# Regrouping the sums of a spectral layer by part, with changes to the order of statistics, evictions and weight preparation

## The chip, the cores and the metric

The kernel runs on one core of one Trainium2 chip. The metric is the device time of one execution in microseconds; the time before is the median of three runs. A profile is one further execution, recorded instruction by instruction. Its time and its span (first to last instruction) are given beside each other below.

The engines are named as in the profile: PE is TensorE's matmuls and PEld its weight loads, DVE is VectorE, ACT is ScalarE, POOL is GpSimd, SP is SyncE, which here only issues DMAs. Each engine runs its instructions in the program's order; semaphores hold an instruction until another engine, or an earlier operation of its own engine, has finished.

## The reference

Two layers over `x` of 2048 rows by 576 columns in bf16, each behind a layer norm without parameters:

```python
h  = x + irfft2(rfft2(layernorm(x)) * (w_r + 1j * w_i), s=(2048, 576))
h2 = h + (gelu(layernorm(h) @ w_gate) * (layernorm(h) @ w_up)) @ w_down
```

The first multiplies the two-dimensional spectrum of the normalised input (2048 by 289, real input) by a complex weight and transforms back. The second is a gated feed-forward layer with 4608 inner columns. `B_x` is not used.

## The kernel before

The core keeps `x` in SBUF as `h_sb`, 128 partitions by 16 rows `h` by 576 columns, so that sequence row 16p + h lies at partition p. The Fourier transform over 2048 rows is split into a part of 16 and a part of 128; the transforms are matmuls with tables of sines and cosines that the kernel makes itself. The source fixes the order of the instructions on every engine; nothing reorders them.

*Head (to about 25 us).* `x` comes in six DMAs (L72 to 74): rows 0-1, 2-3, 4-5, 6-7, 8-11, 12-15. POOL makes index tables (`iota`), DVE and ACT the row table `F16` (L204 to 220, 273 to 279). Row statistics for the first layer norm come from DVE (`sd`, three instructions a row, L117 to 119) for some rows and from ACT (`ln_act`, two passes with accumulation, L124) for the others; `ln_fin` and `ln_rstd` (L128 to 134) finish them on POOL, four rows at a time. `norms(lo, hi)` writes the normalised rows `xn` on DVE (L137) and issues the first transform of each row on PE (`row16`, L298 and L311, into PSUM tiles `f2t` and `f4`). In front of rows 0, 8 and 12 and of the group `pt`, `fill` issues 14, 8, 5 and 3 matmuls whose result is not used (L286). `evict` and `evict4` copy PSUM into `Bt` (L322, L328): all on ACT but the last `evict4`, which DVE does. The column tables `DT`, `DF`, `DI`, `DS` and the tables `TF` (minus sine, cosine, sine for each of nine channels) and its transpose `TI` are made in between. `first` is the part of `TF` for the first two channels, `rest` the part for the other seven.

*Channel loop (25 to 58 us).* `order` lists eight channels k: 1 to 7, then 0. In turn i:

- `f2(c)` transforms columns for c = k and k + 8 (six matmuls, L478) and copies the result to `pq[c]` (L486, ACT; DVE for c = 9).
- `f3(k, half)` combines `pq[k]` and `pq[k + 8]` with `TF` (L493, L494) into `g` (half 0) and `hs` (half 1), copied by ACT (L514).
- `sums_of(k)` makes difference and sum of `g` and `hs` on DVE, `xab` (L523, 524).
- `wmul(k)` multiplies `xab` by the weights `WR` and `WI` (`m1`, `m2`, L541), combines them to `za` and `zb` (L547, 548), and writes the two halves of `Zt` (L552, 553). `sums_of` of the next channel stands between the last two steps. `za`, `zb`, `m1` and `m2` have one buffer each.
- `i3(k, s)`, s = 0, 1, 2, multiplies slices of `Zt` by `TI` (L569, L571; L592 for k = 0) and ACT copies the result to `EO` (L573, L578).

`f2`, `f3` and `i3` take PSUM tiles of one pool, `two`, with four buffers. PE's order in one turn is `f2(k)`, `f3(.,0)`, `i3(.,0)`, `f3(.,1)`, `i3(.,1)`, `f2(k+8)`, `i3(.,2)`, each for a different channel. In the last turn `inv_cols(0, 0)` (L618) stands in place of `f2`, and all three parts of `i3` follow `f3`.

*Weights.* Spectrum rows 0 to 8 of `WR` and `WI` come by DMA (L154), the mirrored rows by an indirect DMA of POOL into `wm` (L381). `WR`'s mirrored part is then copied by a DMA (L411); `WI`'s by DVE with the factor -1 (L452). DVE halves columns 0 and 288 of both (L454).

*Rest.* `inv_cols`, `add_rows`, a second layer norm, and from 72.6 us the feed-forward layer: 144 blocks of 18 matmuls (L876), a Gelu on ACT (L884), a product on DVE (L885), and the down projection (L896).

Of the kernel before, what the change touches and what calls it, by code (L numbers as in the profile page):

```python
# [20 lines left out]
P = 128  # L21
# [20 lines left out]
def kernel_body(  # L42
# [29 lines left out]
    chunks = ((0, 2), (2, 4), (4, 6), (6, 8), (8, 12), (12, 16))  # L72
# [113 lines left out]
    iota(q16[:], [[16, P]])  # L186
# [10 lines left out]
    for t in range(3):  # L197
# [10 lines left out]
    fs = tmp("fs", [P, P], FP32)  # L208
    A.activation(
        fs[:], mu[:].rearrange("p c l -> p (c l)"), ACT.Sin, bias=npib[:], scale=2.0 * PI / P  # L210
    )
    ia, s2a, s2p = tmp("ia", [P, 1]), tmp("s2a", [P, 1], FP32), tmp("s2p", [P, 1], FP32)
    V.tensor_scalar(ia[:], ip[:], 7, None, op0=ALU.bitwise_and)
    V.tensor_scalar(s2a[:], ia[:], 127.0 / 8.0, None, op0=ALU.mult)
    V.scalar_tensor_tensor(s2p[:], ip[:], 0.125, s2a[:], op0=ALU.mult, op1=ALU.add)
    ks = tmp("ks", [P, 9], FP32)
    V.tensor_scalar(ks[:], kv[:], s2p[:, 0:1], None, op0=ALU.mult)
    V.tensor_scalar(iu[:], iu[:], 7, None, op0=ALU.bitwise_and)
    mask = tmp("mask", [P, P], FP32)
    V.tensor_scalar(mask[:], iu[:].rearrange("p c l -> p (c l)"), 0.0, None, op0=ALU.is_equal)  # L220
# [98 lines left out]
    def evict(*hs):  # L319
        for h in hs:  # L320
            n = 1 if h >= H - 2 else 2
            A.copy(  # L322
                Bt[:, 0:4, :].rearrange("p t (c h l) -> p (t c) h l", c=16, h=16)[:, :, h : h + n, :],
                ps_f[h][:, 0:n].rearrange("p h (tc l) -> p tc h l", l=8),
            )

    def evict4(h):
        (V.tensor_copy if h == 12 else A.copy)(  # L328
            Bt[:, 4, :].rearrange("p (c h l) -> p h c l", c=16, h=16)[:, h : h + 4, :, :],
            ps_f["f4", h][:, 0].rearrange("p (h c l) -> p h c l", h=4, c=16),  # L330
        )
# [55 lines left out]
    G.memset(DF[:], 0.0)  # L387
    ln_fin(slice(9, 12, 2))
    sd(8, 10)
# [5 lines left out]
    norms(8, 12)  # L395
    sd(15)
    ln_fin(slice(13, 14))
    ln_rstd(rstd, mv, 12, 16)
# [26 lines left out]
    evict(12, 14, 15)  # L425
# [3 lines left out]
    evict4(12)  # L429
# [19 lines left out]
    sine(rest)  # L449

    def weights():
        V.tensor_scalar(WI[:, 9 : H + 1, 0:J], wm[1][:].rearrange("p (r j) -> p r j", r=8), -1.0, None, op0=ALU.mult)  # L452
        for w in (WR, WI):
            V.tensor_scalar(w[:, :, 0 : J : J - 1], w[:, :, 0 : J : J - 1], 0.5, None, op0=ALU.mult)  # L454

# [4 lines left out]
    pq = {}  # L460
    xab = {}
# [9 lines left out]
    def f2(c):  # L471
        ps = two("pq_ps")
        col = slice(slot[c] * P, (slot[c] + 1) * P)
        steps = [(par, t) for par in range(2) for t in (par, par + 2, 4)]
        if c == order[0]:
            steps.sort(key=lambda s: s[1] == 4)
        for par, t in steps:
            T.matmul(  # L478
                ps[:, par, 0:JP],
                lhsT=Bt[:, t, col],  # L480
                rhs=DT[:, t // 2, par] if t < 4 else DF[:, par],
                start=(t == par),
                stop=(t == 4),
            )
        sb = wk.tile([P, 2, JP], BF16, name="pq", tag="pq", bufs=6)
        (V.tensor_copy if c == 9 else A.copy)(  # L486
            sb[:].rearrange("p r (j a) -> p r j a", a=2),
            ps[:, :, 0:JP].rearrange("p a (r j) -> p r j a", r=2),
        )
        pq[c] = sb  # L490
# [34 lines left out]

    def wmul(k, i, nxt=None):
        x = xab[k]
# [5 lines left out]
        if k:  # L533
            za, zb = (wk.tile([P, 2, JP], BF16, name=n, tag=n, bufs=1) for n in ("za", "zb"))
        else:
            za, zb = zv[:, 0], zv[:, 1]

        for j0, j1 in ((0, J),) if k else ((0, P), (P, J)):
            js = slice(j0, j1)
            for w, m in ((WR, m1), (WI, m2)):  # L540
                V.tensor_tensor(  # L541
                    m[:, :, :, js],
                    x[:, :, :, js],
                    w[:, sl, js].unsqueeze(1).to_broadcast([P, 2, 2, j1 - j0]),
                    ALU.mult,
                )
            V.tensor_tensor(za[:, :, js], m1[:, 0, :, js], m2[:, 1, :, js], ALU.subtract)  # L547
            V.tensor_tensor(zb[:, :, js], m1[:, 1, :, js], m2[:, 0, :, js], ALU.add)
            if nxt:
                sums_of(nxt)  # L550
            if k:
                V.tensor_tensor(zv[:, 0, :, js], za[:, :, js], zb[:, ::-1, js], ALU.add)  # L552
                V.tensor_tensor(zv[:, 1, :, js], zb[:, :, js], za[:, ::-1, js], ALU.subtract)
# [408 lines left out]
```

## Time and profile before

| | us |
|---|---|
| median of 3 runs (503.38 to 503.83) | 503.68 |
| the profiled execution | 503.36 |
| its span | 501.3 |
| PE, DVE, ACT, POOL busy | 491.3, 211.3, 152.6, 28.5 |
| first matmul that is used (L298) starts | 9.10 |
| first column transform (L478) starts | 25.11 |
| first feed-forward matmul (L876) starts | 72.59 |

In a line of the timeline the columns are start, duration, engine, source line, operation, the tile written `<-` the tiles read, shapes, and the number of instructions merged; a bracket gives idle time before it and what ended it. A line of the chain that ended last has start, duration, engine, tile, line. Durations of neighbouring operations overlap a little, so that the distance from start to start is the better measure of cost. The busy time of PE is modelled, and a matmul that waits for its operands inside the engine may count as busy.

### The profile page before, as it was taken

To read this page: it belongs to the slowest core of one execution; us is meant where nothing else is said; L and a number is where in the kernel's file an instruction comes from. 1 tells how busy PE (TensorE), PEld (TensorE's weight loads), DVE (VectorE), ACT (ScalarE), POOL (GpSimd) and SP (SyncE) were. 2 spreads that over 40 slices of the span, in tenths; PEclk is the share of its full clock that TensorE was granted. 3 is DMA by queue.
4 is the path that set the end of the run, shared out by engine and by line. 5 is a ranking of instruction groups with operands and counts; after the bars stand their busy time and mean duration, and the time that the engine had idled before them with its cause. 6 is when DMAs were issued, how large, how long until landed. Compare 5 with 4: busy or idle time off the path is not lost.

```text
span 501.3 us, 9901 instructions
## 1 busy us (share of the span) xinstructions
PE 491.3 (98%) x4340; PEld 290.9 (58%) x4340; DVE 211.3 (42%) x420; ACT 152.6 (30%) x269; POOL 28.5 (6%) x75
## 2 busy tenths in 40 slices
PE   7999999999999999999999999999999999999996
PEld 3567765555567754444477744444677544444775
DVE  8999766788640125433310145333210233333001
ACT  8999972222320012323200032333100133232000
POOL 8500010111110000000000000000000000000000
PEclk9999999999999999999999999999999999999999
DMA  8539686799950049998800099988300688870000
GB/s 283 172 72 198 183 236 160 152 168 189 178 102 1 1 107 184 193 190 155 158 9 0 7 210 203 195 159 151 74 0 1 144 159 159 154 143 1 12 13 26
DMA packets 88104, 61.46 MB, mean 123 GB/s; under 512 B 22781, under 2 KB 86653, under 8 KB 88061
## 3 DMA queue, kind: packets, MB, share of 16 engines
q1 hardware_dynamic: 87773, 59.65, 60.2%
q0 software_dynamic: 288, 1.18, 0.7%
q8 instruction: 34, 0.56, 0.5%
q14 instruction: 9, 0.07, 0.0%
HBM read 52.65 MB, written 2.36 MB: 110 GB/s over the span
## 4 chain that ended last, share of the span: by engine, by line
PE 93%; DVE 3%; ACT 2%; POOL 1%; issue 0%; POOLq 0%
PE gu L876 56%; PE acc L896 28%; PE cs_ps L618 2%; PE pq_ps L478 2%; PE y_ps L741 1%; PE eo_ps L571 1%; PE eo_ps L569 1%; PE gh_ps L494 1%; DVE xn L137 1%; ACT cwb L631 1%; PE gh_ps L493 1%; PE f2t L298 0%; ACT DT L347 0%; ACT Bt L322 0%; POOL kd L198 0%
## 5 line engine op out<-in xcount | busy, mean ns | idle before, releaser
L876 PE MATMUL gu<-Bt,wgu 64*128 64x512 bf16 x2592 | 281.5, 376 | 0.8 <-ACT cwb L631 0.8
L876 PEld LDWEIGHTS <-wgu 64*128 64x128 bf16 x2592 | 130.9, 94 | 148.2 <-issue 1.8
L884 ACT ACTIVATE g_sb<-gu 128x512 f32<-128x512 f32 x144 | 86.0, 597 | 302.8 <-PE gu L876 302.8
L885 DVE TENSOR_TENSOR P_sb<-g_sb,gu 128x512 bf16<-128x512 f32 x144 | 98.6, 685 | 152.9 <-ACT g_sb L884 152.9
L896 PEld LDWEIGHTS <-P_sb 128*128 128x128 bf16 x1152 | 112.4, 98 | 30.6 <-issue 2.4
L896 PE MATMUL acc<-wd,P_sb 128*128 128x288 bf16 x768 | 99.3, 286 | 0.0
L908 DVE TENSOR_TENSOR h_sb<-h_sb,acc 128x576 bf16<-128x576 bf16 x15 | 11.3, 754 | 118.2 <-PE acc L896 118.2
L896 PE MATMUL acc<-wd_a,P_sb 128*128 128x288 bf16 x384 | 52.3, 286 | 0.5 <-DVE h_sb L904 0.5
L478 PE MATMUL pq_ps<-DT,Bt 128*128 128x290 bf16 x64 | 12.2, 286 | 0.0
L286 PE MATMUL f2t<-h_sb,ident 128*128 128x512 bf16 x27 | 8.6, 479 | 3.7 <-DMA h_sb<-in_A_x_dram 3.7
L766 DVE TENSOR_SCALAR hrow<-h_sb,mv,rstd 128x1152 bf16<-128x1152 bf16 x14 | 12.1, 866 | 0.0
L134 POOL TENSOR_TENSOR rstd<-rstd,mhalf 128x1 f32<-128x1 f32 (+1 forms) x16 | 11.4, 713 | 1.3
L618 PEld LDWEIGHTS <-EO 128*128 128x128 bf16 x96 | 9.1, 96 | 3.0 <-issue 0.2
L478 PEld LDWEIGHTS <-Bt 128*128 128x128 bf16 x96 | 9.3, 97 | 2.4
L486 ACT CAST pq<-pq_ps 128x580 bf16<-128x580 f32 x15 | 9.8, 662 | 0.4 <-PE pq_ps L478 0.2
L133 POOL TENSOR_SCALAR rstd<-mv 128x1 f32<-128x1 f32 (+1 forms) x16 | 3.8, 238 | 107.3 <-DVE mv L119 107.0
L298 PE MATMUL f2t<-F,xn 128*128 128x256 bf16 x64 | 9.3, 275 | 0.7 <-DVE xn L137 0.7
L124 ACT ACTIVATE junk<-h_sb 128x576 bf16<-128x576 bf16 x14 | 9.4, 676 | 0.5 <-DMA h_sb<-in_A_x_dram 0.5
L118 DVE BATCH_NORM_STATS2 st<-h_sb 128x6 f32<-128x288 bf16 x21 | 9.3, 441 | 0.0
L117 DVE BATCH_NORM_STATS2 st<-h_sb 128x6 f32<-128x288 bf16 x21 | 9.3, 441 | 0.0
L618 PE MATMUL cs_ps<-DI,EO 128*128 128x290 bf16 x32 | 9.1, 285 | 0.0
L493 PE MATMUL gh_ps<-pq,TF 128*128 128x289 bf16 x32 | 8.7, 286 | 0.3 <-ACT TF L256 0.3
(132 smaller groups left out, 248.8 us busy)
## 6 DMA issues: line engine op xcount, KB each, us to landing
wgu<-in_B_w_gate_dram SPq DMA_DIRECT2D x48, 432.0 KB, 5.3
wgu<-in_B_w_up_dram SPq DMA_DIRECT2D x48, 432.0 KB, 6.8
wd<-in_B_w_down_dram SPq DMA_DIRECT2D x2, 1728.0 KB, 7.5
wd_a<-in_B_w_down_dram SPq DMA_DIRECT2D x1, 1728.0 KB
out_dram<-h_sb SPq DMA_DIRECT2D x3, 576.0 KB, 3.4
h_sb<-in_A_x_dram SPq DMA_DIRECT2D x4, 288.0 KB, 3.2
h_sb<-in_A_x_dram SPq DMA_DIRECT2D x2, 576.0 KB, 6.3
WR<-in_A_w_r_dram SPq DMA_DIRECT2D x1, 650.2 KB
```

The source lines that it names most:

```text
L124: A.activation(junk[:], h_sb[:, h, :], fn, scale=sc, accum_out=mv[:, h, i : i + 1])
L134: G.tensor_tensor(dst[:, sl], dst[:, sl], mhalf[:, sl], ALU.pow)
L478: T.matmul(ps[:, par, 0:JP], lhsT=Bt[:, t, col], rhs=DT[:, t // 2, par] if t < 4 else DF[:, par], start=(t == par), stop=(t == 4),)
L486: (V.tensor_copy if c == 9 else A.copy)(sb[:].rearrange("p r (j a) -> p r j a", a=2), ps[:, :, 0:JP].rearrange("p a (r j) -> p r j a", r=2),)
L493: T.matmul(dst, lhsT=TF[:, ts[k1], t0, :], rhs=a, start=True, stop=False)
L618: T.matmul(ps[:, e, 0:JP], lhsT=EO[x][:, 2 * e + jt if jt < 2 else 4, 2 * g : 2 * g + 2].rearrange("p h e k l -> p (h e k l)"), rhs=DI[:, ...
L766: V.tensor_scalar(hrow[:], h_sb[:, h, :].rearrange("p (r k) -> p r k", k=64).unsqueeze(2).to_broadcast([P, NR, 2, 64]), mv2[:, h, 0:1], rs ...
L876: T.matmul(gu[:, c, :], lhsT=w[rows, r, i * P : (i + 1) * P], rhs=hl[tcnk % 2][rows, r, :], start=(r == 0), stop=(r == NR - 1),)
L884: A.activation(g_sb[:], gu[:, 0, :], ACT.Gelu_apprx_tanh)
L885: V.tensor_tensor(p_sb(fa + i), g_sb[:], gu[:, 1, :], ALU.mult)
L896: T.matmul(acc[:, c, 0:DH], lhsT=p_sb(f)[:, st * P : (st + 1) * P], rhs=wd[f // NWA][:, f % NWA, cc], start=(f == 0), stop=(f == NFT - 1),)
L908: V.tensor_tensor(hv, hv, acc[:, :, 0:DH], ALU.add)
```

## The change

The diff has these parts.

1. *Input.* The first DMA of `x` is split in two, rows 0 and 1 (seven DMAs in all).
2. *Row table.* ACT makes three sine tables (the third with the opposite sign) in two instructions, and one DVE operation compares and multiplies, where a mask, a product and a negation stood. The scaling of `q16`, `s2p`, `ks` is spread otherwise, with two small DVE operations fewer.
3. *Order of statistics.* ACT takes row 0 in place of row 1, DVE rows 1, 2, 4, 6 and 8 ahead of `norms(0, 4)`, where it took 0, 2, 4 and 6. `sd(10)` is left of `sd(8, 10)`. `ln_rstd(12, 16)` is done in three pieces, row 13 last; the memset of `DF` and `minus_sine(first)` move.
4. *Late evictions.* `evict(14)` goes to DVE, `evict4(12)` to ACT.
5. *Weights.* `WI`'s mirrored part is copied by a DMA like `WR`'s; no factor -1. POOL, not DVE, halves the two columns, in the head.
6. *Pairing by part.* Each half of `f3` makes, for one of the two parts r, the pair that was spread over both halves; the signs that this turns are those that the factor -1 had turned. The two `Zt` operations of a channel now write columns `zv[:, :, 0]` and `zv[:, :, 1]`, and the parts s of `i3` use these in turn: s = 0 reads only the first.
7. *One operation moved.* The second `Zt` operation of a channel is held back and issued behind the two weight products of the next channel (`held`, `release`).
8. *Order in a turn.* `f2` no longer copies; `f2_out` does. PE's order is `f2(k)`, `f3(.,0)`, `i3(.,0)`, `f3(.,1)`, `f2(k+8)`, `i3(.,1)`, `i3(.,2)`. DVE copies `pq[9]` in two halves. `sine(rest)` moves behind the copy of `pq[1]`, and the copy of `pq[2]` behind `f3(1, 1)`.

The core of it:

```diff
-    chunks = ((0, 2), (2, 4), (4, 6), (6, 8), (8, 12), (12, 16))
+    chunks = ((0, 1), (1, 2), (2, 4), (4, 6), (6, 8), (8, 12), (12, 16))
...
     def row_table():
-        V.tensor_tensor(
-            F16[:, 0:2, :],
-            fs[:].unsqueeze(1).to_broadcast([P, 2, P]),
-            mask[:].unsqueeze(1).to_broadcast([P, 2, P]),
-            ALU.mult,
-        )
-        V.tensor_scalar(F16[:, 2, :], F16[:, 0, :], -1.0, None, op0=ALU.mult)
+        V.scalar_tensor_tensor(
+            F16[:],
+            iu[:].rearrange("p c l -> p (c l)").unsqueeze(1).to_broadcast([P, 3, P]),
+            0.0,
+            fs[:],
+            op0=ALU.is_equal,
+            op1=ALU.mult,
+        )
...
-    ln_act(1)
+    ln_act(0)
     ln_act(3)
-    sd(0)
     row_table()
-    sd(2)
-    ln_fin(slice(1, 4, 2))
+    sd(1, 2)
+    ln_fin(slice(0, 4, 3))
     ln_rstd(rstd, mv, 0, 4)
-    sd(4, 6)
+    sd(4, 6, 8)
     norms(0, 4)
...
-    sd(8, 10)
+    sd(10)
...
     norms(8, 12)
+    minus_sine(first)
+    G.memset(DF[:], 0.0)
     sd(15)
+    ln_rstd(rstd, mv, 12, 13)
+    ln_rstd(rstd, mv, 14, 16)
     ln_fin(slice(13, 14))
-    ln_rstd(rstd, mv, 12, 16)
+    ln_rstd(rstd, mv, 13, 14)
...
-    nc.sync.dma_start(WR[:, 9 : H + 1, 0:J], wm[0][:].rearrange("p (r j) -> p r j", r=8))
+    for w, t in ((WR, wm[0]), (WI, wm[1])):
+        nc.sync.dma_start(w[:, 9 : H + 1, 0:J], t[:].rearrange("p (r j) -> p r j", r=8))
+    for w in (WR, WI):
+        G.tensor_scalar(w[:, :, 0 : J : J - 1], w[:, :, 0 : J : J - 1], 0.5, None, op0=ALU.mult)
...
-    evict(12, 14, 15)
+    evict(12, 15)
+    evict4(12)
...
-    evict4(12)
+    evict(14, copy=V.tensor_copy)
...
-        for r in range(2):
-            if half:
-                comb(ps[:, 1 - r, 0:J], k, C, q[:, r, 0:J], NS, p[:, r, 0:J])
-            else:
-                comb(ps[:, r, 0:J], k, C, p[:, r, 0:J], SN, q[:, r, 0:J])
+        r = half
+        comb(ps[:, r, 0:J], k, C, p[:, r, 0:J], SN, q[:, r, 0:J])
+        comb(ps[:, 1 - r, 0:J], k, C, q[:, r, 0:J], NS, p[:, r, 0:J])
...
+    def release(n):
+        for _ in range(min(n, len(held))):
+            V.tensor_tensor(*held.pop(0))
...
+        if k:
+            times(WR, m1, js)
+            times(WI, m2, js)
+            release(1)
+            za, zb = (wk.tile([P, 2, JP], BF16, name=n, tag=n, bufs=1) for n in ("za", "zb"))
+            parts(za, zb, js)
+            held.append((zv[:, :, 0, js], za[:, :, js], zb[:, ::-1, js], ALU.add))
+            held.append((zv[:, :, 1, js], zb[:, :, js], za[:, ::-1, js], ALU.subtract))
             if nxt:
                 sums_of(nxt)
-            if k:
-                V.tensor_tensor(zv[:, 0, :, js], za[:, :, js], zb[:, ::-1, js], ALU.add)
-                V.tensor_tensor(zv[:, 1, :, js], zb[:, :, js], za[:, ::-1, js], ALU.subtract)
+                release(1)
+            return
...
-        if i >= 3 and not last:
-            i3(order[i - 3], 1)
         if not last and i:
             f2(order[i] + 8)
+            f2_out(order[i] + 8)
         if i >= 3:
-            for jt in range(0 if last else 2, NJT):
+            for jt in range(0 if last else 1, NJT):
                 i3(order[i - 3], jt)
```

More of the change, by code (lines that the diff above doesn't have):

```diff
@@ L185, in kernel_body @@
     q16 = tmp("q16", [P, P], FP32)
-    iota(q16[:], [[16, P]])
+    iota(q16[:], [[2, P]])
     make_identity(nc, ident[:])
@@ L207, in kernel_body @@
     V.tensor_scalar(mu[:], mu[:], 127, None, op0=ALU.bitwise_and)
-    fs = tmp("fs", [P, P], FP32)
-    A.activation(
-        fs[:], mu[:].rearrange("p c l -> p (c l)"), ACT.Sin, bias=npib[:], scale=2.0 * PI / P
-    )
[L212 to L215, printed above, removed]
+    fs = tmp("fs", [P, 3, P], FP32)
+    for n, bias, sign in ((slice(0, 2), npib, 1.0), (slice(2, 3), pib, -1.0)):
+        A.activation(
+            fs[:, n],
+            mu[:].rearrange("p c l -> p (c l)").unsqueeze(1).to_broadcast([P, n.stop - n.start, P]),
+            ACT.Sin,
+            bias=bias[:],
+            scale=sign * 2.0 * PI / P,
+        )
+    V.tensor_scalar(iu[:], iu[:], 7, None, op0=ALU.bitwise_and)
+    s2p = tmp("s2p", [P, 1], FP32)
+    V.scalar_tensor_tensor(s2p[:], iu[:, 0, 0:1], 127.0, ip[:], op0=ALU.mult, op1=ALU.add)
     ks = tmp("ks", [P, 9], FP32)
[L217 to L220, printed above, removed]
+    V.tensor_scalar(ks[:], kv[:], s2p[:, 0:1], 0.125, op0=ALU.mult, op1=ALU.mult)
     def drop_sign(dst, src):
@@ L317, in row16_rest, with evict @@
             )
-    def evict(*hs):
+    def evict(*hs, copy=A.copy):
         for h in hs:
             n = 1 if h >= H - 2 else 2
-            A.copy(
+            copy(
                 Bt[:, 0:4, :].rearrange("p t (c h l) -> p (t c) h l", c=16, h=16)[:, :, h : h + n, :],
@@ L327, in evict4 @@
     def evict4(h):
-        (V.tensor_copy if h == 12 else A.copy)(
+        A.copy(
             Bt[:, 4, :].rearrange("p (c h l) -> p h c l", c=16, h=16)[:, h : h + 4, :, :],
@@ L386, in kernel_body @@
         )
-    G.memset(DF[:], 0.0)
     ln_fin(slice(9, 12, 2))
-    sd(8, 10)
+    sd(10)
     ln_rstd(rstd, mv, 8, 12)
@@ L448, in kernel_body @@
         )
[L449 to L454, printed above, removed]
     xn_pool.__exit__(None, None, None)
@@ L460, in kernel_body @@
     pq = {}
+    pq_ps = {}
     xab = {}
@@ L484, in f2, with f2_out @@
             )
[L485 to L488, printed above, removed]
+        pq[c] = wk.tile([P, 2, JP], BF16, name="pq", tag="pq", bufs=6)
+        pq_ps[c] = ps
+    def f2_out(c, copy=A.copy, rs=slice(0, 2)):
+        copy(
+            pq[c][:, rs].rearrange("p r (j a) -> p r j a", a=2),
+            pq_ps[c][:, :, 0:JP].rearrange("p a (r j) -> p r j a", r=2)[:, rs],
         )
-        pq[c] = sb
     def comb(dst, k1, t0, a, t1, b):
@@ L524, in sums_of @@
         V.tensor_tensor(x[:, 1, ::-1, 0:J], g[:, :, 0:J], hs[:, :, 0:J], ALU.add)
+    held = []
+    def release(n):
+        for _ in range(min(n, len(held))):
+            V.tensor_tensor(*held.pop(0))
     def wmul(k, i, nxt=None):
@@ L650, in kernel_body @@
             f2(order[i])
+            if i != 1:
+                f2_out(order[i])
         if i == 0:
+            sine(rest)
             f2(order[0] + 8)
+            for r in range(2):
+                f2_out(order[0] + 8, V.tensor_copy, slice(r, r + 1))
             angle_c(rest)
             minus_sine(rest)
-            weights()
         if last:
@@ L665, in kernel_body @@
             if i == 1:
+                f2_out(order[1])
                 sums_of(order[0])
```

29 lines of the change are left out of this document (15 added, 14 removed).

## The prediction

> **What bounds the kernel now.** I read the list of cores first (granted clock 1.000, so no throttling to explain), then the busy shares, the chain that ended last, the timeline by stage, and the landing times of the input.
>
> ```profile
> span 501.3 us, 9901 instructions
> ...
> PE 491.3 (98%) x4340; PEld 290.9 (58%) x4340; DVE 211.3 (42%) x420; ACT 152.6 (30%) x269; POOL 28.5 (6%) x75
> ...
> PE gu L876 56%; PE acc L896 28%; PE cs_ps L618 2%; PE pq_ps L478 2%; PE y_ps L741 1%; PE eo_ps L571 1%; PE eo_ps L569 1%; PE gh_ps L494 1%; DVE xn L137 1%; ACT cwb L631 1%; PE gh_ps L493 1%; PE f2t L298 0%; ACT DT L347 0%; ACT Bt L322 0%; POOL kd L198 0%
> ```
>
> 84% of the chain is the feed-forward part (L876, L896), which starts at 72.59 us and which the diff does not touch. So the change is worth what it moves that start. Everything it edits lies before 58.3 us; from there (L592) on, both programs do the same.
>
> The chain to row 0's normalisation, and the landing of the input that will matter (of the two input DMAs in this answer, issued at 2.1 and 2.6, only the second, rows 8 to 11, has a landing recorded):
>
> ```profile
> 6.55 0.13 POOL rev L172
> ...
> 7.53 1.06 POOL rstd L134
> 8.59 0.03 issue
> 8.61 1.45 DVE xn L137 x4
> ```
>
> ```profile
> L74 SPq DMA_DIRECT2D h_sb<-in_A_x_dram x2: 432/432/432, 2.1 to 2.6; - x2
> ...
> DMA to landing us min/median/max: 5.8/5.8/5.8
> ```
>
> Row 0 waits for POOL, busy without a break since 0.84, and rows 8 to 11 land at 2.6 + 5.8 = 8.4 us. From xn on, TensorE and ACT pass the start time along: ACT evicts row pair 0 at 10.47, when TensorE ends row 1, and then has no idle time until 19.76.
>
> In the channel loop, DVE's timeline over one turn (start, duration):
>
> ```profile
> 37.67 0.76 DVE L541 TENSOR_TENSOR m<-xab,WR 128x1156 bf16<-128x1156 bf16 x1
> 38.34 0.76 DVE L541 TENSOR_TENSOR m<-xab,WI 128x1156 bf16<-128x1156 bf16 x1
> 39.13 0.47 DVE L547 TENSOR_TENSOR za<-m,m 128x578 bf16<-128x578 bf16 x1
> 39.51 0.46 DVE L548 TENSOR_TENSOR zb<-m,m 128x578 bf16<-128x578 bf16 x1
> 39.88 0.46 DVE L523 TENSOR_TENSOR xab<-g,hs 128x578 bf16<-128x578 bf16 x1
> 40.25 0.46 DVE L524 TENSOR_TENSOR xab<-g,hs 128x578 bf16<-128x578 bf16 x1
> 40.62 0.46 DVE L552 TENSOR_TENSOR Zt<-za,zb 128x578 bf16<-128x578 bf16 x1
> 40.99 0.46 DVE L553 TENSOR_TENSOR Zt<-zb,za 128x578 bf16<-128x578 bf16 x1
> 41.37 0.76 DVE L541 TENSOR_TENSOR m<-xab,WR 128x1156 bf16<-128x1156 bf16 x1
> ```
>
> DVE has no gap: a turn is 41.37 - 37.67 = 3.70 us, and TensorE's turns (first column transform of a turn at 36.34, 40.05) are as long. An operation that needs nothing of its neighbour starts 0.67 (large) or 0.37 us (small) after it, which is less than its 0.76 or 0.46 of duration; za, which needs the product just made, comes 0.79 after it. TensorE's own work per turn is less: two transforms of 0.74, eight matmuls of 0.122 (L493/494) and ten of 0.11 (L569/571), 3.56 us; ACT's, start to start, about 3.3.
>
> **The change, part by part.** T is the start of xn for row 0 (8.61 now), X that of the first column transform (25.11 now).
>
> *Head.* The order of the built program puts three statistics, rows 4, 6 and 8, ahead of xn on DVE, where two stood. DVE runs in order. The new row table is one operation of 128x384; nearest rows are 0.48 (128x256, L236) and 1.14 (128x896), so about 0.6, against 0.23 + 0.37 + 0.40 for the mask and two operations now. The two sines need 0.53 + 0.40 on ACT by the rows of 256 and 128 elements, so DVE starts the table near 3.7 and rows 1, 2, 4 and 6 (0.93 each, 7.43 to 8.36) near 4.2; it is free near 7.9. Row 8 then waits for its landing. The DMAs in front of it are the same bytes, with one more issue (0.47 us); the stream runs at 311 to 383 GB/s from 4 us on, so I take 8.5 (8.4 to 8.87, and 7.9 if it should land before DVE is free). T = 8.5 + 0.05 + 0.93 = 9.48, 0.87 later. POOL's rstd (8.58) is then no longer last. The one statistic saved later on DVE (0.93, between 12.77 and 16.51) makes DVE break even for row 8, but TensorE does not: rows 0 to 7 take it 5.75 us from the first xn and the eight warm-up matmuls 1.9. It recovers only its 0.19 us wait at 16.95, ACT its 0.21 at 19.76; I count 0.17 of these. So X = 25.11 + 0.87 - 0.17 = 25.81. The late evictions do not move it: TensorE reaches X through the pt group, which waits for the eviction of rows 12 and 13 alone (23.99 to 24.04); the others end by then on either engine. Row 13's rstd, now a POOL step of its own, ends near 21.8 instead of 20.84; TensorE asks for row 13 at 22.3, so that is covered, by 0.1.
>
> *From X to the first sums.* The sine moves behind the copy of pq 1, and pq 9 is copied in two halves, of which the first transform half needs only one: TensorE's 0.11 us at 27.61 goes. What ended last before the sums (29.39) were hs at 29.36 and the weight operations at 29.35 together, so taking 0.75 + 0.20 + 0.22 of weight work off DVE gives nothing beyond hs, which is 0.11 earlier. The first sums start at X + 4.17 (now X + 4.28). On POOL the two halvings (34 elements; rows from 0.24 to 0.92) end near 25, and m needs them at 30.8; the extra DMA for WI (0.73 to issue, 4.3 to land, as WR's) likewise.
>
> *Loop.* Pairing by part makes the first half of the inverse need only one Zt operation, and pq's second copy no longer stands behind the 1.02 us copy of EO: TensorE's waits of 0.15 a turn (L494 at 37.35, 41.00) go. But that engine is not the bound; DVE does the same eight operations. The held Zt operation now fills the place between m and za, which looks like a gain of 0.79 - 0.67 = 0.12. It is not: za and zb have one buffer each, the held operation still reads them, and in the built program the new za waits for that very operation. A small operation after which a dependent one follows is spaced 0.49 (xab at 29.77, m at 30.26) or 0.56 (zb at 54.31, Zt at 54.87) instead of 0.37; I take 0.52. The turn becomes 0.67 + 0.67 + 0.52 + 0.38 + 4 x 0.37 = 3.72. The wait has moved, not gone.
>
> *Tail.* Five turns later m of channel 7 starts at X + 4.17 + 0.87 + 3.33 + 5 x 3.72 = X + 26.97. Only after it and its partner (0.67 each) comes the held half of channel 6, done 0.46 + 0.03 later: X + 28.80. TensorE, in order, wants it at about X + 27.9, with nothing else to do: a stall of about 0.9 that does not exist now (both halves were ready 0.36 ahead). From there it has 0.66 + 1.49 + 1.10 + 1.49 = 4.74 to L592: X + 33.54, against 58.25 - 25.11 = X + 33.14 now. Channel 0's Zt, near X + 32.8, is in time.
>
> **Sum.** +0.70 (head) + 0.40 (X to L592, all of the loop and tail) = +1.10. The profiled execution took 503.36 (span 501.30 and 2.06 around it): 504.46; it lies 0.32 under the median shown (503.68), so **504.8** as a median.
>
> **Rivals.**
> 1. *Not slower: the head costs nothing.* Rows 8 to 11 would have to land before DVE asks, at 7.9: T = 8.9, X = 25.23, in all +0.12 + 0.40 = 504.2; with T unchanged, 503.9. For it: the first DMAs are halves and queue earlier. Against: 8.4 by the landing row, and a stream already full. It decides at a landing under about 8.0. 13%.
> 2. *The held operation pays.* If za did not wait, the turn would be TensorE's, 3.57; the stall at channel 6 shrinks to 0.38 and L592 comes at X + 32.8: +0.70 - 0.34 = 504.0. Against: the wait stands in the program. 15%. With rival 1 as well it is 503.4 or less; 5% for gains beyond 0.2%, the rest of "faster" being errors of mine.
> 3. *TensorE falls to half rate* while it waits some 1.1 us for row 0. The warm-up matmuls are 0.43 us apart until 8.31, then 0.24, so such a rate exists; 4.6 us at it, as at the start, are 3.6 rows of 1.29 instead of 0.72: about +2.0 more, 506.8. No idle time of that length stands in this trace after 3.7. 7%.
>
> [...]
>
> [...]
>
> **Chances and range.** Forecast 60%, rivals 13, 15 and 7, 5 for a gain. The measurement tells about 0.2% (1.0 us) from no change. The forecast lies just past that line (504.69); its unknowns (landing 8.4 to 8.87: -0.1 to +0.37; dependent spacing 0.49 to 0.56: -0.2 to +0.2; POOL and ACT close behind in the head) lean upwards. So slower 0.50, same 0.40, faster 0.10. The range takes in both rivals towards no change and the dearest landing and spacing, but not rival 3: 503.5 to 505.8.
>
> **What would show it.** After: xn of row 0 near 9.5, behind a DVE wait for an input DMA (right) or near 8.6 behind POOL (rival 1); L478's first near 25.8; m to m 3.7 with za 0.5 behind the held Zt (right) or 3.57 (rival 2); a TensorE wait of 0.8 to 0.9 for Zt in the second half of channel 6, a little after 54; the first gate matmul near 73.7. It is wrong if the head moves by less than 0.4, or if TensorE shows no such stall.

## The result, and the profile after

The changed kernel takes **506.89 us** (median of 4 runs: 507.41, 506.34, 507.37, 506.42) against 503.53 for the kernel before on the same chip: a ratio of 1.0066, 95% interval 1.0049 to 1.0084. It is slower by some 3.4 us, where the forecast had 1.1 and a range that ended at 505.8. The profiled execution is the one of 507.41, with a span of 505.6. The runs of 507.41 and 507.37 have a mean granted clock of 0.993, those of 506.42 and 506.34 one of 0.997 and 1.000, so the two quicker ones are still 2.8 us or more slower than the kernel before, with little or no time at a reduced clock on record.

The page of the changed kernel, the lines that answer to those of before (span, busy time, shares of the chain that ended last):

```profile
span 505.6 us, 9912 instructions
...
PE 492.5 (97%) x4340; PEld 292.0 (58%) x4340; DVE 210.8 (42%) x414; ACT 153.8 (30%) x270; POOL 30.7 (6%) x81
...
PE gu L900 55%; PE acc L920 28%; DVE m L546 2%; PE cs_ps L639 1%; DVE Zt L532 1%; PE y_ps L765 1%; DMA Bt<-hrow 1%; DVE za L551 1%; DVE h_sb L810 1%; DVE xab L526 0%; DVE zb L552 0%; DVE xab L525 0%; PE eo_ps L613 0%; PE eo_ps L590 0%; DVE hrow L790 0%
```

The feed-forward part (L900, L920) is as long as before; it starts later, at 76.91 instead of 72.59. Marking T (row 0's normalisation on DVE) and X (the first column transform) as the prediction does:

| start, us | before | forecast | after |
|---|---|---|---|
| T | 8.61 | 9.48 | 10.40 |
| X | 25.11 | 25.81 | 28.90 |
| first sums, from X | +4.28 | +4.17 | +4.15 |
| last inverse matmuls, L613 (before L592), from X | +33.14 | +33.54 | +33.51 |
| first gate matmul | 72.59 | 73.7 | 76.91 |

So what was mis-sized lies in the head, ahead of X: it moved X by 3.79 us in this run, where the forecast had 0.70. Everything from X to L613 came out within 0.03 us of its sum. (0.16 more stand between L613 and the gate; why is open.) The number of the line L613 differs in the other kernels; below it stands for this line in each.

Three views of the changed kernel show the head. DVE's timeline, around its wait for row 8:

```profile
7.41 0.44 DVE L118 BATCH_NORM_STATS2 st<-h_sb 128x6 f32<-128x288 bf16 x1
7.88 0.21 DVE L119 BATCH_NORM_AGGREGATE mv<-st 128x2 f32<-128x12 f32 x1
9.43 0.46 DVE L117 BATCH_NORM_STATS2 st<-h_sb 128x6 f32<-128x288 bf16 x1 [1.33 <-DMA h_sb<-in_A_x_dram]
9.80 0.44 DVE L118 BATCH_NORM_STATS2 st<-h_sb 128x6 f32<-128x288 bf16 x1
10.28 0.21 DVE L119 BATCH_NORM_AGGREGATE mv<-st 128x2 f32<-128x12 f32 x1
10.40 1.44 DVE L137 TENSOR_SCALAR xn<-h_sb,mv,rstd 128x576 bf16<-128x576 bf16 x4
```

Rows 8 to 11 land only at 9.43; the forecast had 8.5. DVE stands still for 1.33 us in front of row 8, and row 0, whose rstd POOL had finished near 8.6, comes after it. The table by stretch (stretch, its length, then busy time of PE, PEld, DVE, ACT, POOL, granted clock, DMA share, GB/s):

```profile
6.00:7.00 1.00, 1.00 (x5) 0.34 (x4) 0.94 (x4) 1.00 (x4) 0.92 (x4) 1.00 0.74 210
7.00:8.00 1.00, 1.00 (x5) 0.29 (x3) 0.97 (x4) 1.00 (x5) 0.82 (x3) 1.00 0.82 281
8.00:9.00 1.00, 0.02 (x1) 0.00 (x0) 0.09 (x1) 1.00 (x4) 0.78 (x2) 1.00 0.97 382
9.00:10.00 1.00, 0.00 (x0) 0.00 (x0) 0.57 (x2) 0.85 (x3) 0.42 (x2) 1.00 1.05 388
10.00:11.00 1.00, 0.12 (x1) 0.12 (x2) 0.97 (x4) 0.93 (x4) 0.92 (x1) 0.59 1.09 336
11.00:12.00 1.00, 1.00 (x6) 0.44 (x5) 1.00 (x4) 0.00 (x0) 0.88 (x2) 0.50 1.16 327
...
16.00:17.00 1.00, 1.00 (x7) 0.41 (x6) 0.97 (x5) 1.00 (x2) 0.92 (x2) 0.50 0.83 324
17.00:18.00 1.00, 1.00 (x11) 0.68 (x10) 0.97 (x4) 1.00 (x3) 1.00 (x3) 1.00 0.34 135
```

Between 6 and 8 us the DMA engines moved 210 and 281 GB/s, where the forecast had counted on 311 to 383. TensorE is empty from 8.02 to 10.88, and at about 10.2 its granted clock falls to a half, until 17.0. What that does is in its timeline (some rows of `xn`, one line each, in which four matmuls are merged):

```profile
10.88 1.04 PE L301 MATMUL f2t<-F,xn 128*128 128x256 bf16 x4 [2.86 <-DVE xn L137]
...
12.10 1.03 PE L301 MATMUL f2t<-F,xn 128*128 128x256 bf16 x4
...
15.73 1.03 PE L301 MATMUL f2t<-F,xn 128*128 128x256 bf16 x4
...
16.95 0.62 PE L301 MATMUL f2t<-F,xn 128*128 128x256 bf16 x4
...
17.68 0.61 PE L301 MATMUL f2t<-F,xn 128*128 128x256 bf16 x4
```

The rows are 1.21 us apart until 16.95, and 0.72 after that. This is rival 3, which had 7%, though after a wait of 2.86 us and not of the 1.1 that it named.

The loop's turn on DVE, and TensorE at channel 6's second half, answer to the steps of the forecast that held:

```profile
37.31 0.76 DVE L546 TENSOR_TENSOR m<-xab,WR 128x1156 bf16<-128x1156 bf16 x1
37.98 0.76 DVE L546 TENSOR_TENSOR m<-xab,WI 128x1156 bf16<-128x1156 bf16 x1
38.66 0.46 DVE L532 TENSOR_TENSOR Zt<-zb,za 128x578 bf16<-128x578 bf16 x1
39.15 0.47 DVE L551 TENSOR_TENSOR za<-m,m 128x578 bf16<-128x578 bf16 x1
39.52 0.46 DVE L552 TENSOR_TENSOR zb<-m,m 128x578 bf16<-128x578 bf16 x1
...
40.64 0.46 DVE L532 TENSOR_TENSOR Zt<-za,zb 128x578 bf16<-128x578 bf16 x1
41.01 0.76 DVE L546 TENSOR_TENSOR m<-xab,WR 128x1156 bf16<-128x1156 bf16 x1
```

The turn is 41.01 - 37.31 = 3.70; the held `Zt` operation (38.66) takes the place behind the two products, and `za` follows it after 0.49, not 0.37.

```profile
56.70 0.27 PE L592 MATMUL eo_ps<-TI,Zt 128*128 128x256 bf16 x1
57.67 0.28 PE L590 MATMUL eo_ps<-TI,Zt 128*128 128x256 bf16 x1 [0.69 <-DVE Zt L532]
```

TensorE's matmuls are 0.11 apart, but here 0.97: it waits for the held operation of channel 6, as foretold (about 0.9).

### The profile page after: what moved, and what is told of

It is laid out like the page before. It is cut to its first block, busy times and chain, and to the rows that moved or that the text cites. A ratio compares the mean times of both kernels' runs of the same rounds, so it can differ in the third digit from the quotient of the medians.

```text
span 505.6 us, 9912 instructions
## 1 busy us (share of the span) xinstructions
PE 492.5 (97%) x4340; PEld 292.0 (58%) x4340; DVE 210.8 (42%) x414; ACT 153.8 (30%) x270; POOL 30.7 (6%) x81
## 4 chain that ended last, share of the span: by engine, by line
PE 86%; DVE 6%; DMA 1%; issue 0%
PE gu L900 55%; PE acc L920 28%; DVE m L546 2%; PE cs_ps L639 1%; DVE Zt L532 1%; PE y_ps L765 1%; DMA Bt<-hrow 1%; DVE za L551 1%; DVE h_sb L810 1%; DVE xab L526 0%; DVE zb L552 0%; DVE xab L525 0%; PE eo_ps L613 0%; PE eo_ps L590 0%; DVE hrow L790 0%
## 5 line engine op out<-in xcount | busy, mean ns | idle before, releaser
L900 PE MATMUL gu<-Bt,wgu 64*128 64x512 bf16 x2592 | 281.5, 376 | 1.0 <-DMA Bt<-hrow 1.0
L900 PEld LDWEIGHTS <-wgu 64*128 64x128 bf16 x2592 | 131.2, 94 | 148.1 <-issue 2.0
L920 PEld LDWEIGHTS <-P_sb 128*128 128x128 bf16 x1152 | 112.4, 98 | 30.6 <-issue 2.4
L920 PE MATMUL acc<-wd,P_sb 128*128 128x288 bf16 x768 | 99.3, 286 | 0.0
L920 PE MATMUL acc<-wd_a,P_sb 128*128 128x288 bf16 x384 | 52.3, 286 | 0.5 <-DVE h_sb L928 0.5
L301 PE MATMUL f2t<-F,xn 128*128 128x256 bf16 x64 | 11.4, 318 | 2.9 <-DVE xn L137 2.9
L134 POOL TENSOR_TENSOR rstd<-rstd,mhalf 128x1 f32<-128x1 f32 (+2 forms) x18 | 12.1, 674 | 1.5
L133 POOL TENSOR_SCALAR rstd<-mv 128x1 f32<-128x1 f32 (+2 forms) x18 | 4.4, 242 | 108.7 <-DVE mv L119 108.3
L301 PEld LDWEIGHTS <-xn 128*128 128x128 bf16 x64 | 6.0, 108 | 5.7 <-DVE xn L137 3.4
```

What stands on the lines that cost most here:

```text
L134: G.tensor_tensor(dst[:, sl], dst[:, sl], mhalf[:, sl], ALU.pow)
L301: T.matmul(f2t[:, b, t * 2 * P : (t + 1) * 2 * P], lhsT=x[:, d0 : d0 + P], rhs=F16[:, n : n + 2, :], start=(n == 0), stop=(n == 1),)
L900: T.matmul(gu[:, c, :], lhsT=w[rows, r, i * P : (i + 1) * P], rhs=hl[tcnk % 2][rows, r, :], start=(r == 0), stop=(r == NR - 1),)
L920: T.matmul(acc[:, c, 0:DH], lhsT=p_sb(f)[:, st * P : (st + 1) * P], rhs=wd[f // NWA][:, f % NWA, cc], start=(f == 0), stop=(f == NFT - 1),)
```

## The experiments

Each time is a median beside the kernel before on the same chip (503.75 in the first two groups, 503.42 in the third, 503.49 in the last). "Old head" and "old late head" mean the order that the kernel before has.

| run | T | X | median | ratio, 95% interval |
|---|---|---|---|---|
| first_dma_whole | 9.66 | 26.93 | 505.00 | 1.0028 (1.0019 to 1.0037) |
| row8_late | 8.69 | 26.89 | 505.45 | 1.0035 (1.0022 to 1.0049) |
| fill26 | 10.41 | 27.56 | 506.06 | 1.0046 (1.0033 to 1.0060) |
| old_order | 8.67 | 26.67 | 505.50 | 1.0034 (1.0021 to 1.0046) |
| late_undone | 10.14 | 27.59 | 506.97 | 1.0076 (1.0062 to 1.0090) |
| old_head | 8.67 | 25.82 | 504.29 | 1.0010 (1.0001 to 1.0019) |
| before_rstd3 | 8.62 | 26.56 | 504.90 | 1.0025 (1.0015 to 1.0035) |
| before_early | 10.82 | 28.52 | 506.86 | 1.0064 (1.0050 to 1.0078) |
| before_order | 9.69 | 26.48 | 504.70 | 1.0020 (1.0011 to 1.0029) |
| before_split | 8.70 | 25.73 | 504.38 | 1.0016 (1.0006 to 1.0025) |
| before_fill8 | 8.61 | 27.19 | 504.94 | 1.0027 (1.0018 to 1.0036) |
| loop_two_buffers | 8.90 | 25.86 | 503.18 | 0.9996 (0.9987 to 1.0005) |
| loop_ch6_early | 8.66 | 25.27 | 503.63 | 1.0006 (0.9997 to 1.0015) |
| loop_both | 8.66 | 26.32 | 502.93 | 0.9989 (0.9979 to 0.9998) |
| loop_no_hold | 8.68 | 25.27 | 503.13 | 0.9996 (0.9987 to 1.0005) |

T and X are of one profiled execution each. X scatters by about half a microsecond from run to run in the kernels with the old late head (last section), so small differences are read from the medians.

### First group: one part of the head undone, on the changed kernel

**first_dma_whole**

```diff
-    chunks = ((0, 1), (1, 2), (2, 4), (4, 6), (6, 8), (8, 12), (12, 16))
+    chunks = ((0, 2), (2, 4), (4, 6), (6, 8), (8, 12), (12, 16))
```

> The changed kernel with its input in six DMAs as before (rows 0 and 1 in one). Theory A (the split of the first DMA makes rows 8 to 11 land late, and DVE's early row 8 waits for that landing): they land near 8.4 again, row 0's normalisation starts near 9.5 and the first column transform near 25.8, granted clock 1.000, time 504.6 to 505.2. Rival (the landing is late for another reason, the split has no part in it): landing stays near 9.4, row 0 at 10.4, TensorE waits for it, time 506.0 or more.

Its stretches from 6 to 8, and DVE's wait for row 8:

```profile
6.00:7.00 1.00, 1.00 (x4) 0.30 (x2) 0.97 (x5) 1.00 (x4) 0.92 (x4) 1.00 1.06 403
7.00:8.00 1.00, 1.00 (x4) 0.33 (x3) 0.91 (x4) 1.00 (x5) 0.82 (x3) 1.00 0.96 346
```

```profile
8.68 0.46 DVE L117 BATCH_NORM_STATS2 st<-h_sb 128x6 f32<-128x288 bf16 x1 [0.73 <-DMA h_sb<-in_A_x_dram]
```

The stream is back at 403 and 346 GB/s and rows 8 to 11 land at 8.68 instead of 9.43. TensorE waits 0.98 us, its clock stays full, and the time falls by 1.9. No run of this kernel (504.75 to 505.54) reaches those of the changed kernel (506.34 to 507.41). So the split of the first DMA makes this cost, and in these profiles it goes with the late landing: between 6 and 7 us the stream moves 189 to 253 GB/s in the changed kernel, fill26, late_undone, before_early and before_split, which have the split, and 353 to 403 in the kernel before, first_dma_whole, before_order and before_fill8, which do not. The landing scatters even so: in loop_two_buffers, with the first DMA whole, ACT waits for row 9 until 9.60. The time is as expected, but X is not: 26.93, not 25.8. Something else costs more than a microsecond.

**row8_late**

```diff
-    sd(4, 6, 8)
+    sd(4, 6)
...
-    sd(10)
+    sd(8, 10)
```

> The changed kernel with the statistic of row 8 moved back to row 10's (split first DMA kept). Theory A: whatever the landing does, row 0 no longer waits for it: row 0 near 8.6 behind POOL's rstd, no time at half clock, first column transform near 25.1; what is left is loop and tail, so 503.8 to 504.3. Rival (the later landing costs in another place, rows 9 on ACT and the rows 8 to 11 on TensorE): row 0 near 8.6, but the time stays over 505.

T is back at 8.69, yet X is at 26.89 and the time 505.45. The forecast's only head term was removed, and 1.7 us remained. Theory A, that the early wait is all, falls here. The rival's time (over 505) came true, but not at the place that it named: in the trace TensorE waits 1.52 us at row 13, as in first_dma_whole, fill26 and old_order.

**fill26**

```diff
-        fill(f2t[:, b, :], {0: 14, 8: 8, 12: 5}.get(h, 0))
+        fill(f2t[:, b, :], {0: 26, 8: 8, 12: 5}.get(h, 0))
```

> The changed kernel with 26 warm-up matmuls ahead of row 0 instead of 14, which fill TensorE's wait from 8.0 to 10.9. Theory A (the clock falls because TensorE idles 2.9 us there): row 0 stays at 10.4, no slice is at half clock in any run, the mean granted clock is 1.000 in all of them, and the time is that of the better runs of the changed kernel, 505.5 to 506.4, never 507.4. Rival (the clock falls for a reason that idling has no part in): slices at 0.5 stay, and some runs are at 507.4 with a mean clock of 0.993.

```profile
10.88 0.61 PE L301 MATMUL f2t<-F,xn 128*128 128x256 bf16 x4 [0.65 <-DVE xn L137]
...
11.60 0.61 PE L301 MATMUL f2t<-F,xn 128*128 128x256 bf16 x4
```

With TensorE kept busy (idle 0.65 us before row 0), T is still 10.41, but the clock is 1.000 in every run and the rows are 0.72 apart. In the profiles X comes 1.34 earlier than in the changed kernel; the medians differ by 0.8, the ratios by 1.0. That is the price of the half rate. The cause is TensorE's idling, 2.86 us in the changed kernel.

**old_order**

```diff
-    ln_act(0)
+    ln_act(1)
     ln_act(3)
-    row_table()
-    sd(1, 2)
-    ln_fin(slice(0, 4, 3))
+    sd(0)
+    row_table()
+    sd(2)
+    ln_fin(slice(1, 4, 2))
...
-    sd(4, 6, 8)
+    sd(4, 6)
...
-    sd(10)
+    sd(8, 10)
```

(with the input in six DMAs)

> The changed kernel with the input DMAs and the early order of statistics as before (rows 0, 2, 4, 6 on DVE, 1 and 3 on ACT, row 8 with row 10); row table, weights, late evictions, pairing, held operation and order of turns stay changed. Theory A with the loop's sum as predicted: first column transform at 25.1 to 25.3, DVE's turn 3.70 to 3.72, TensorE waits 0.7 to 0.9 at channel 6's second half, L613 at X + 33.5: 503.7 to 504.1, ratio 1.0004 to 1.0012. Rival (the held operation pays): 503.0 or less. Rival (the late head, row 13's rstd and the dealt evictions, costs as well): first column transform at 25.8 or later, over 504.4.

505.50: the third case of the expectation. In its trace DVE waits 1.05 us for POOL's rstd of row 13, TensorE 1.52 us behind it. This made theory B: the late head costs too.

### Second group: the late head, and the parts alone

**late_undone**

```diff
-    ln_rstd(rstd, mv, 12, 13)
-    ln_rstd(rstd, mv, 14, 16)
-    ln_fin(slice(13, 14))
-    ln_rstd(rstd, mv, 13, 14)
+    ln_fin(slice(13, 14))
+    ln_rstd(rstd, mv, 12, 16)
...
-    evict(12, 15)
-    evict4(12)
+    evict(12, 14, 15)
...
-    evict(14, copy=V.tensor_copy)
+    evict4(12)
```

(minus sine and the memset of `DF` also back in their places)

> The changed kernel with the late head as before: rstd of rows 12 to 15 in one POOL operation behind row 15's statistic, row pair 14 on ACT and the last f4 tile on DVE, minus sine and the memset of DF in their old places. The early head keeps its split DMA and DVE's early row 8. Theory B (two costs that overlap: the early wait for the landing, and row 13's rstd as the last of four POOL steps, 22.4 instead of 20.8, which stops TensorE 1.5 us): row 0 still at 10.4; where the clock stays full, the first column transform comes near 26.7 (1.79 of the wait less 0.2) and the time is 505.3 to 505.7; where it falls to half, TensorE and not POOL is last at row 13 and the time stays 507.2 to 507.5. Rival A (the late head is covered, all is the early wait): no gain against the changed kernel at either clock, 506.4 and 507.4.

No gain: 506.97 against 506.89. No run had a full clock (0.993 to 0.997), so only the half-clock part of the expectation could be tested. It had 507.2 to 507.5; the runs lie from 506.3 to 507.9, no lower than those of the changed kernel. That TensorE's slow rows and not POOL would be last there is not what the profiled run shows (506.32, one stretch at half rate): POOL stands idle for 2.38 us until ACT's statistic for row 13, its power of four columns ends at 23.03, and TensorE waits 0.42 us behind it. In the changed kernel row 13's rstd, the last piece, ends at 23.39. Behind the early head, the old late head ends late as well.

**old_head**: the edits of old_order and late_undone together.

> The changed kernel with the early head (input DMAs, order of statistics) and the late head as before; row table, weights, pairing, held operation and order of turns stay changed. Theory B: first column transform back at 25.0 to 25.2, L613 at X + 33.5, all that is left is loop and tail, 0.3 to 0.5: 504.0 to 504.3 against 503.7, ratio 1.0006 to 1.0011. Rival (the row table or the halving on POOL costs in the head too): first column transform at 25.5 or later, over 504.5. Rival (the paired loop gains): 503.4 or less.

1.0010, or 0.54 us: what loop and tail cost. L613 at X + 33.49, as in the changed kernel (33.51), and the TensorE wait at channel 6 (0.70). The profiled run's X (25.82) belongs to the later of the two groups that the last section describes.

**before_rstd3**: the four lines of rstd from late_undone's diff, put into the kernel before.

> The kernel before with one edit: rstd of rows 12 to 15 in three pieces as in the changed kernel, row 13 last. Theory B: POOL ends row 13 near 22.4, DVE waits about 1 us for it, the first column transform comes 1.2 to 1.5 later, and 504.9 to 505.3, ratio 1.0024 to 1.003. Rival A (covered, as predicted): less than 0.2 later, ratio 1.0004 or less.

1.0025, with medians 1.15 us apart, from this edit alone. POOL's, DVE's and TensorE's timelines:

```profile
19.09 0.39 POOL L133 TENSOR_SCALAR rstd<-mv 128x2 f32<-128x2 f32 x1 [1.65 <-DVE mv L119]
19.57 0.83 POOL L134 TENSOR_TENSOR rstd<-rstd,mhalf 128x2 f32<-128x2 f32 x1
20.37 0.58 POOL L128 TENSOR_TENSOR sq<-mv 128x1 f32<-128x1 f32 x1
21.03 0.26 POOL L129 TENSOR_TENSOR mv<-mv,sq 128x1 f32<-128x1 f32 x1
21.38 0.22 POOL L133 TENSOR_SCALAR rstd<-mv 128x1 f32<-128x1 f32 x1
21.68 0.58 POOL L134 TENSOR_TENSOR rstd<-rstd,mhalf 128x1 f32<-128x1 f32 x1
```

```profile
20.82 0.43 DVE L137 TENSOR_SCALAR xn<-h_sb,mv,rstd 128x576 bf16<-128x576 bf16 x1
22.30 1.75 DVE L137 TENSOR_SCALAR xn<-h_sb,mv,rstd 128x576 bf16<-128x576 bf16 x3 [1.05 <-POOL rstd L134]
```

```profile
21.30 0.61 PE L298 MATMUL f2t<-F,xn 128*128 128x256 bf16 x4
23.43 0.83 PE L298 MATMUL f2t<-F,xn 128*128 128x256 bf16 x6 [1.52 <-DVE xn L137]
```

In the kernel before, one power served all four rows:

```profile
19.46 1.38 POOL L134 TENSOR_TENSOR rstd<-rstd,mhalf 128x4 f32<-128x4 f32 x1
```

Row 13 is last of six POOL operations, which begin only when row 15's statistic is there (19.09, behind 1.65 us of idle time). Cutting this POOL operation did not divide its time: the power took 0.58 for one column and 0.83 for two, where it takes 1.04 (before_early, before_fill8) to 1.38 for four. Row 13 is ready at 22.3 instead of 20.9, and TensorE, which wanted it at 21.9, stops for 1.52 us.

**before_early**: the split DMA and the early order, put into the kernel before.

> The kernel before with the early edits alone: split first DMA, ACT's row 0 for row 1, DVE's rows 1, 2, 4, 6, 8 ahead of row 0's normalisation. Theory B: rows 8 to 11 land near 9.4, row 0 at 10.4, TensorE waits 1.8 to 2.9 us; the first column transform 1.6 later at full clock (505.1 to 505.5) and 3.5 to 3.8 later where the clock falls (507). Rival (as predicted): landing 8.5, row 0 at 9.5, first column transform 0.7 later, 504.3 to 504.5.

1.0064, nearly the whole loss. Row 8 waits until 9.84, T is 10.82, TensorE is idle for 2.43 us, and the clock is 0.993 to 0.997 in all runs. Landing and T are 0.4 later than the expectation had them; the time is near the 507 that it had for a falling clock.

### Third group: the loop, with the old head

**loop_two_buffers**

```diff
-            za, zb = (wk.tile([P, 2, JP], BF16, name=n, tag=n, bufs=1) for n in ("za", "zb"))
+            za, zb = (wk.tile([P, 2, JP], BF16, name=n, tag=n, bufs=2) for n in ("za", "zb"))
```

> The kernel old_head (changed loop, old head) with two buffers each for za and zb, so that za no longer waits for the held Zt operation that still reads them. Theory B (the one buffer is the wait, as the forecast had it): m2 to held Zt 0.67, held Zt to za 0.37, turn 0.67 + 0.67 + 6 x 0.37 = 3.57 against 3.70, five turns 0.65 earlier, TensorE (3.56 of own work) just keeps up: L613 0.5 to 0.65 earlier, 503.6 to 503.8 against old_head's 504.3, about 503.7 of the kernel before. [...]

DVE's turn:

```profile
37.82 0.76 DVE L544 TENSOR_TENSOR m<-xab,WR 128x1156 bf16<-128x1156 bf16 x1
38.50 0.76 DVE L544 TENSOR_TENSOR m<-xab,WI 128x1156 bf16<-128x1156 bf16 x1
39.17 0.46 DVE L530 TENSOR_TENSOR Zt<-zb,za 128x578 bf16<-128x578 bf16 x1
39.54 0.46 DVE L549 TENSOR_TENSOR za<-m,m 128x578 bf16<-128x578 bf16 x1
39.91 0.46 DVE L550 TENSOR_TENSOR zb<-m,m 128x578 bf16<-128x578 bf16 x1
...
41.02 0.46 DVE L530 TENSOR_TENSOR Zt<-za,zb 128x578 bf16<-128x578 bf16 x1
41.39 0.76 DVE L544 TENSOR_TENSOR m<-xab,WR 128x1156 bf16<-128x1156 bf16 x1
```

41.39 - 37.82 = 3.57, and `za` starts 0.37 behind the held operation. L613 comes at X + 32.85, 0.64 earlier than in old_head. The ratio is 0.7 us below old_head's, as expected. The single buffer was the wait: with the second one the held operation to `za` takes 0.37 like the other operations of 0.46 that do not read each other, with one buffer it takes 0.49 (old_head, 39.26 to 39.75).

**loop_ch6_early**

```diff
                 sums_of(nxt)
-                release(1)
+                release(2 if k == order[5] else 1)
```

> The kernel old_head with channel 6's second Zt operation issued at once, not held behind channel 7's two weight products. Theory B (the 0.4 of loop and tail is the stall of 0.7 to 1.0 at channel 6's second half, the only place where TensorE waits for a held operation): the stall goes or falls below 0.3, L613 at X + 32.8 to 33.1, 503.6 to 503.9. Rival (the 0.4 comes from the turns): the stall goes but L613 stays at X + 33.4 or later, 504.2 or more.

The wait at channel 6 is gone, L613 comes at X + 33.13, 0.36 earlier, and the time is 0.2 us lower by the ratios, whose intervals overlap, so that the gain stands in the trace and not in the times. It falls just short of what was expected (X + 32.8 to 33.1): the operation now pushes channel 7's products back by 0.38 (48.46 to 52.54 in place of 3.70), and TensorE waits 0.33 for channel 7's first half instead.

**loop_both**: both edits.

> Both edits: two buffers for za and zb, and channel 6 not held. Theory B: 0.65 from the turns and 0.3 to 0.7 from the stall, less what TensorE's own 3.56 a turn does not give back: L613 at X + 32.2 to X + 32.6, 503.0 to 503.5, at or just under the kernel before (503.75). [...]

L613 at X + 32.48 and 502.93: 0.9989 of the kernel before, with an interval that just leaves out 1. It is the only version here whose interval lies below 1.

**loop_no_hold**

```diff
             if nxt:
                 sums_of(nxt)
-                release(1)
+            release(2)
             return
```

> The kernel old_head with nothing held: both Zt operations of a channel at the end of its own turn, as before; pairing by part, order of turns and weights stay changed. Theory B (the held operation buys nothing with one buffer and costs the stall at channel 6): DVE's turn 3.70 as before, no stall over 0.3 at channel 6, L613 at X + 33.0, 503.7 to 503.9, ratio 1.000 to 1.0004. Rival (the pairing or the order of turns is what costs): 504.2 or more.

The turn is 3.70, nothing stalls, L613 comes at X + 32.81, better than expected (33.0) and than before (33.14); 0.9996. So with one buffer the held operation costs 0.7 and buys nothing. All else that the diff changes behind X (pairing by part, the order of a turn, the weights) gains 0.33 in the trace, 0.14 of it ahead of the first sums (X + 4.14 against X + 4.28); no run takes these apart, and the interval of the times (0.9987 to 1.0005) takes in no gain.

### Fourth group: the early head's parts, each alone on the kernel before

**before_order**: the early order of statistics, six DMAs.

> The kernel before with the early order of statistics alone (ACT row 0, DVE rows 1, 2, 4, 6, 8 ahead of row 0's normalisation), the input in six DMAs. Theory B (the order costs what the forecast said, if the landing holds): landing near 8.5, row 0 at 9.5 to 9.7, TensorE idle for about 1 us, clock full, first column transform 0.7 to 0.9 later, 0.7 to 0.9 over the kernel before, ratio 1.0014 to 1.0018. Rival (the order itself makes the landing late): row 0 at 10 or later, 1.5 us or more over.

1.0020, or 1.2 us, where 0.7 to 0.9 was expected. T is 9.69 without a wait: DVE has no gap up to it. Here DVE's own statistics, and not the landing, hold row 0 back, and the time shows nothing of the 1.08 recovered before X.

**before_split**: the split DMA alone.

> The kernel before with the first input DMA split alone. Theory B (the split makes rows 8 to 11 land near 9.1 to 9.8, but nothing in the old order needs them before 9.0): ACT waits for row 9 by up to 0.8 us, TensorE's warm-up ends up to 0.7 earlier and it idles up to 1 us more, row 0 at 8.6; 0 to 0.5 over the kernel before. Rival (the split costs by itself): 1 us or more over.

1.0016, or 0.9 us; 0 to 0.5 was expected. ACT waits 0.54 for row 5 at 5.42 and is 0.3 later from then on; row 13's chain on POOL moves back with it, and DVE waits 0.28 for rstd at 21.26. What makes up the rest is open.

**before_fill8**

```diff
-        fill(f2t[:, b, :], {0: 14, 8: 8, 12: 5}.get(h, 0))
+        fill(f2t[:, b, :], {0: 8, 8: 8, 12: 5}.get(h, 0))
```

> The kernel before with 8 warm-up matmuls ahead of row 0 instead of 14: TensorE ends them near 7.2 and idles 1.9 us before row 0, which stays at 8.6; nothing else is changed. Theory B (an idle time of some 1.7 us or more is enough for the clock to fall to half, for one stretch of 3.4 us or two): slices at 0.5 between 8 and 15, rows 1.2 us apart in them, 1.0 to 1.8 over the kernel before in those runs. [...]

1.0027, with T unchanged at 8.61. TensorE's warm-up and rows:

```profile
3.61 3.57 PE L286 MATMUL f2t<-h_sb,ident 128*128 128x512 bf16 x8 [3.61 <-DMA h_sb<-in_A_x_dram]
9.10 1.04 PE L298 MATMUL f2t<-F,xn 128*128 128x256 bf16 x4 [1.91 <-DVE xn L137]
...
10.31 1.03 PE L298 MATMUL f2t<-F,xn 128*128 128x256 bf16 x4
...
13.95 1.03 PE L298 MATMUL f2t<-F,xn 128*128 128x256 bf16 x4
...
15.96 0.61 PE L298 MATMUL f2t<-F,xn 128*128 128x256 bf16 x4
```

The rows run at half rate until about 15.2, though the column of the granted clock shows 1.00 all through. Theory B is not right for this run: the rate did not fall, it had never risen. The eight matmuls (0.43 apart, half rate) ended at 7.18, before any rise; in the kernel before, the rise comes at 8.3, within the fourteen. So eight warm-up matmuls in place of fourteen alone were enough for slow rows (1.21 us apart, 0.72 from 15.96 on); how little idling brings a full clock down, this run does not tell.

## Why the prediction was wrong, point by point

**The head, +0.70: the step that failed.** X moved by 3.79 us in the profiled run, and some 2.8 of the loss in the medians lie in the head (3.4 less the 0.5 of old_head). Three terms were undersized.

- *The landing, "I take 8.5".* Measured 9.43 (9.16 and 9.84 in late_undone and before_early), 8.68 with the first DMA whole. The working argued that the same bytes with one more issue keep the rate of 311 to 383 GB/s; the split stream ran at 189 to 253 between 6 and 7 us in the five profiles named under first_dma_whole (210 here, 403 with the first DMA whole). The cost of the smaller first DMAs was bounded at 0.37 and turned out as 0.5 to 1.2 against the 8.68. The bound came from one profile, and the landing scatters by more than that (8.68 and, in loop_two_buffers, 9.60 with the first DMA whole). Why the rate sinks with the split is open.
- *The wait, "rival 3, 7%".* The forecast had TensorE idle for about 1.1 us, and a wait of 0.98 (first_dma_whole) or 1.13 (row8_late) did nothing to the clock. But a landing 0.9 later, with a warm-up that began 0.7 earlier on the smaller DMA, made 2.86. The half rate that followed costs 0.8 to 1.3 (fill26); the rival had 2.0.
- *Row 13's rstd, "covered, by 0.1".* Alone it costs 1.15 us (before_rstd3). It was placed at 21.8; it ends at 22.3 with T where it was before. The six operations take 3.2 us in a row, and none of them starts before row 15's statistic. In the profiled changed kernel it is hidden: TensorE's slow rows reach row 13 later than POOL does, and TensorE has no wait there. Undoing it gained nothing in late_undone, where the old order is late as well.

Of "I count 0.17" as recovered, before_order shows nothing, but its interval (0.55 to 1.5 us) is too wide to settle so little. The parts alone (1.2 order, 0.9 split, 1.15 rstd, 0.5 loop) sum to 3.8; the whole is 3.4. With half a microsecond of doubt on each part this says only that they account for the loss, not how they overlap.

**X to the first sums, -0.11:** measured -0.13. Right.

**The loop, turn 3.72:** measured 3.70, with `za` 0.49 behind the held operation, where 0.52 was taken. The wait had moved, not gone, and loop_two_buffers shows that the buffer is the reason. **Rival 2** was right in its mechanism, 3.57, where the wait is really taken away.

**The tail, a stall of about 0.9, L613 at X + 33.54:** 0.97 start to start (0.86 over the normal 0.11) and X + 33.51. Right; loop_ch6_early shows what it is worth.

**Rival 1** (the head costs nothing) is out. **Rival 3** came true in its mechanism, by the recorded clock in three of the four runs, after a wait that the forecast did not see coming. That its 506.8 lies beside the measured 506.89 is luck: its 2.0 for the half rate was too much, and without the half rate the kernel stands at 506.06 (fill26) and not at the 504.8 that it was added to. The 7% was the author's estimate, from a trace in which TensorE has no such wait after 3.7. The half-rate stretches were 6.8 us in the changed kernel (10.2 to 17.0) and 3.4 in before_early (11.8 to 15.2) and late_undone (11.9 to 15.3; all worked out from the mean clock of the stretches). The clock fell in the profiled runs with waits of 2.86, 2.43 and 1.75 us ahead of row 0 (in the changed kernel 2.2 us into the wait), while 1.52 (before_rstd3) and 1.58 (loop_both, ahead of row 12) left the rate full. What decides between them, no run tells.

## What to carry to other kernels

When an operation is moved up on an engine that runs in order, write down what it will wait for and what stands behind it, and price that wait at the worst landing that any similar stream shows (9.84 in before_early, where 8.5 was taken), not at the mean rate; then ask what the waiting engines lose besides time, as TensorE's rows were 1.21 us apart instead of 0.72 here after a wait of 2.86. The pieces of a small POOL operation cost far more than their share here (0.58 us for one column, 1.04 to 1.38 for four), so count every piece, from the latest input of the first. Ask of an operation put into a gap whether it shares a buffer with what comes next: here the turn took 3.70 with one buffer and 3.57 with two, 0.13 us a turn.

## What was not expected of the hardware

The granted clock's column did not show every slow stretch: before_fill8 ran five rows at 1.21 us each, and later ones at 0.72, with the column at 1.00 all through. Here the distance from start to start of like matmuls was the surer reading.

Most runs of the kernel before fall into two groups of times, half a microsecond apart (503.2 to 503.5 and 503.7 to 503.9). In the profiles of this kernel and of those with its late head whose T is 8.6 to 8.7 and whose rows run at full rate, POOL's subtraction for row 13 takes 0.19 us in some, and X is 25.1 to 25.3; in the others it takes 0.46 to 0.54, and X is 25.7 to 26.3. In old_head it takes 0.53 and in the kernel before 0.19, though in both it begins 0.01 us ahead of DVE's first f32 operation on `pd`. So the start alone does not tell the groups apart. What makes the difference, no run tells.
